# Summing the sixteen planes of the next batch's keys: plain loads with adds on GpSimd and VectorE in place of accumulating transfers

## Chip, core and metric

One core of a Trainium2 chip. The metric is the device time of one execution in microseconds (us); three runs of the kernel before took 972.6 to 973.67 us, median 973.59. PE is TensorE, DVE is VectorE, ACT is ScalarE, POOL is GpSimd, SP is SyncE (which here only issues transfers).

## What is computed

The reference, cut to what matters. B = 4 batches of N = 12288 queries, C = 128 channels, 768 pooled keys per batch; then a soft mixture of experts over all 49152 rows.

```python
kv_pool = kv.reshape(B, H // 4, 4, W // 4, 4, C).mean(axis=(2, 4))   # 16 planes are averaged
k = v = kv_pool.reshape(B, -1, C) @ w_sr                             # 768 keys per batch
s = scale * (q @ k.transpose(0, 2, 1)); a = softmax(s); x = a @ v    # attention
logits = x @ phi                                                     # 32 slots
d = softmax over rows of logits; slot_input = d.T @ x
slot_out = expert MLP of slot_input                                  # 8 experts, 1024 wide
out = softmax over slots of logits @ slot_out
```

## The kernel before

Queries are worked in **tiles** of 128, 12 tiles to a **group** (G), 8 groups and so 96 tiles (TB) to a batch, 32 groups in all. Per tile PE makes the scores `s` from keys and queries that are split into a high and a low part (`khi`, `klo`, `qhi`, `qlo`: three matmuls for each half of the 768 keys, lines 385 to 387), DVE takes the row maximum (391), ACT the exponential `p` (400). Half of `p` is transposed on DVE (424), half is split into two 16-bit parts by ACT (407) and POOL (411) into a buffer `hl` and transposed by a DMA that SP issues (420, tile `pb`). Per group PE turns the transposed `p` into logits (456, then 468, which needs `pb`), and, once the group's weights `D` have come through POOL, ACT and POOL (546, 562, 570), multiplies `p` by them (585: 96 matmuls in six blocks T0 to T5). The logits of 16 groups stay in one tile `LL`; the first 16 groups' logits are spilled by SP after use.

**Keys of a batch.** The 16 planes of 128x768 numbers are summed, and the sum gives `khi`/`klo` through PE (268), ACT (271) and DVE (275), the tables `us`, `vu`, `vb` and `selb` for the logits through PE (283), DVE (290 to 294), ACT (299) and so on, a transposition `put` on PE (312), and `V96` through PE (328) and ACT (331). This is the key stage, `kv_ops`. Batch 0's planes are loaded at the start and added by DVE (`add0`, `sum0`, `fin0`). For batches 1 to 3 `kv_acc` works while the batch ahead is being computed: SP loads plane 0 into two free slots of `LL`, and POOL issues fifteen transfers of 384 KB, one for each further plane, that add to what lies there; each waits until the one before it has landed.

**Order.** PE, DVE, ACT and POOL run their instructions in the order in which the plan emits them. Every operation has a key, the tile count `at` of its group plus a number from the table `TAU` for its kind, raised to just above the keys of what it depends on, and operations are emitted by ascending key. One unit of the key is one tile. SP's transfers go out in emission order too. In the table of before `kv1` to `kv15` lie between 24.91 and 91.518 of a batch's 96 units and `kmm0`, the key stage's first matmul, at 95.981, on the border to the next batch.

```python
    def op(self, eng, kind, at, deps, fn, acq=(), use=()):
        key = at + TAU.get(kind, 0.0)
        for d in deps:
            key = max(key, self.ops[d][2] + 1e-4)
```

Scores, key matmuls and logits share three buffers of two PSUM banks each (`ss`, ring "s").

Of the kernel before, what the change touches and what calls it, by code (L numbers as in the profile page):

```python
# [14 lines left out]
ALU = mybir.AluOpType  # L15
# [40 lines left out]
    "mcol": 21.441, "mmm": 21.883, "csum7": 22.133, "mred": 22.329, "dsub": 22.579, "xho12": 22.858, "dexp": 23.18,  # L56
# [3 lines left out]
    "xho15": 30.893, "bsum": 31.358, "kv3": 31.519, "dal": 31.805, "xh8": 31.827, "umax": 32.854, "csub": 33.213,  # L60
# [988 lines left out]
```

## Time and profile before

| what | value |
|---|---|
| median of three runs | 973.59 us |
| the profiled execution's own time | 982.6 us |
| its span, first to last instruction | 980.8 us |
| busy: PE, DVE, ACT, POOL | 873.0, 788.5, 661.3, 659.9 us |
| POOL's accumulating issues | 45, 41.1 us of POOL |
| queue that SP feeds / that POOL feeds, share of 16 DMA engines | 71.7% / 12.0% |

The span has three stages: the start until the first group is through (73 us), 30 further groups until 853 us, and the end with the experts and the output. "Busy" of PE counts matmuls that overlap one another; how fast PE goes is read from when instructions start. The profiled execution is 9.0 us longer than the median of the runs without a profile.

### The profile page before, as it was taken

How to read it: one execution, taken by the hardware profiler on the slowest of the kernel's cores; microseconds unless marked ns; L12 is line 12 of the kernel's file. 1: busy time of each engine (PE TensorE's matmuls, PEld its weight loads, DVE VectorE, ACT ScalarE, POOL GpSimd, SP SyncE). 2: the span in 40 equal slices, each digit the busy share in tenths (PEclk: the TensorE clock that was granted, in tenths of full speed). 3: DMA queues.
4: the chain of work that ended last, by engine and by line, in shares of the span. 5: the costliest groups of instructions: out<-in, count | busy, mean ns of one | idle time of the engine just before them, and what ended most of it. 6: DMA issues, size and time to landing. Idle time of an engine off the chain costs nothing. (4 is left out here: it accounts for less than half of the span.)

```text
span 980.8 us, 27134 instructions
## 1 busy us (share of the span) xinstructions
PE 873.0 (89%) x10436; PEld 618.0 (63%) x10436; DVE 788.5 (80%) x1496; ACT 661.3 (67%) x1244; POOL 659.9 (67%) x795
## 2 busy tenths in 40 slices
PE   1789998998998999998999999989999999866763
PEld 1677675775776766666767767757777777632341
DVE  6778886887887787887888878868998888847665
ACT  1677776776886776776877777857877888711333
POOL 0468886785788786785777877866776777747400
PEclk9999998999999999999999999999999999978567
DMA  7379999697789999895699999885666767693788
GB/s 300 64 147 179 178 174 171 130 169 136 132 160 171 166 178 163 146 163 101 143 179 175 166 176 151 159 142 104 133 130 129 131 130 131 107 335 161 319 347 362
DMA packets 338289, 167.61 MB, mean 171 GB/s; under 512 B 310768, under 2 KB 313072, under 8 KB 338032
## 3 DMA queue, kind: packets, MB, share of 16 engines
q1 hardware_dynamic: 331248, 148.04, 71.7%
q0 software_dynamic: 6480, 17.70, 12.0%
q8 instruction: 82, 1.34, 0.6%
q14 instruction: 47, 0.39, 0.1%
q10 hardware_dynamic: 432, 0.15, 0.1%
HBM read 62.01 MB, written 28.31 MB: 92 GB/s over the span
## 5 line engine op out<-in xcount | busy, mean ns | idle before, releaser
L411 POOL TENSOR_TENSOR hl<-p,hl 128x384 f16<-128x384 f32 x384 | 353.3, 962 | 97.1 <-issue 52.5
L400 ACT ACTIVATE p<-s,nm 128x768 f32<-128x768 f32 x384 | 344.5, 897 | 105.6 <-DVE nm L392 100.8
L391 DVE TENSOR_REDUCE nm<-s 128x1 f32<-128x768 f32 x384 | 364.4, 949 | 48.6 <-PE s L387 48.0
L385 PE MATMUL s<-khi,qhi 128*128 128x384 f32 x768 | 284.3, 370 | 7.3 <-ACT p L400 7.3
L387 PE MATMUL s<-khi,qlo 128*128 128x384 f32 x768 | 261.2, 340 | 0.1
L386 PE MATMUL s<-klo,qhi 128*128 128x384 f32 x768 | 260.8, 340 | 0.0
L385 PEld LDWEIGHTS s<-khi,qhi 128*128 128x128 f32 x768 | 146.0, 190 | 83.9 <-issue 65.2
L424 DVE STREAM_TRANSPOSE pa<-p 128x768 f32<-128x768 f32 x192 | 179.3, 958 | 0.0
L407 ACT ACTIVATE hl<-p 128x768 f16<-128x768 f32 x192 | 158.1, 836 | 29.5 <-DMA pb<-hl 25.1
L585 PE MATMUL m<-p,D 128*32 128x192 f32 x3072 | 168.0, 340 | 6.8 <-POOL D L570 4.4
L369 POOL TENSOR_TENSOR qlo<-q,qhi 128x512 fp32r<-128x512 f32 x96 | 132.4, 1379 | 56.6 <-ACT qhi L365 55.5
L386 PEld LDWEIGHTS s<-klo,qhi 128*128 128x128 f32 x768 | 146.6, 191 | 0.1
L387 PEld LDWEIGHTS s<-khi,qlo 128*128 128x128 f32 x768 | 146.2, 190 | 0.4 <-POOL qlo L369 0.4
L585 PEld LDWEIGHTS m<-p,D 128*32 128x32 f32 x3072 | 82.9, 111 | 67.0 <-issue 30.2
L456 PE MATMUL lq<-pa,vu 32*32 32x384 f32 x3072 | 88.5, 491 | 1.9 <-DVE pa L424 1.9
L400 ACT ACTIVATION_READ_ACCUMULATOR p<-s,nm 128x1 f32 x384 | 74.2, 193 | 0.0
L392 DVE TENSOR_SCALAR nm<-nm 128x1 f32<-128x1 f32 x384 | 59.1, 154 | 13.2
L479 DVE COPY lps<-lq 128x768 f32<-128x768 f32 x32 | 30.6, 958 | 47.8 <-PE lq L468 47.8
L468 PE MATMUL lq<-pb,vb 128*32 128x384 f16 x1152 | 54.7, 334 | 15.8 <-DMA pb<-hl 8.6
L456 PEld LDWEIGHTS lq<-pa,vu 32*32 32x32 f32 x3072 | 45.5, 103 | 32.5 <-issue 14.0
L365 ACT ACTIVATE qhi<-q 128x512 fp32r<-128x512 f32 x96 | 59.7, 621 | 2.0 <-PE s L386 2.0
L979 PE MATMUL po<-ct,sl 32*128 32x384 f32 x192 | 38.7, 739 | 24.5 <-DVE ct L973 24.1
(120 smaller groups left out, 736.5 us busy)
## 6 DMA issues: line engine op xcount, KB each, us to landing
q<-qT SPq DMA_DIRECT2D x96, 256.0 KB, 3.3
outT<-o SPq DMA_DIRECT2D x32, 768.0 KB, 4.4
LL<-kvT POOLq DMA_DIRECT2D x45, 384.0 KB, 6.1
raw<-kv SPq DMA_DIRECT2D x8, 768.0 KB, 11.6
pb<-hl SPq DMA_TRANSPOSE x384, 3.6
w_p<-w SPq DMA_DIRECT2D x6, 768.0 KB, 6.6
pa<-w SPq DMA_DIRECT2D x1, 3328.0 KB, 15.4
spill<-LL SPq DMA_DIRECT2D x16, 192.0 KB, 2.1
```

The lines of the kernel that those rows point to most:

```text
L365: nc.scalar.activation(qsp[i][0], src, AF.Copy)
L369: nc.gpsimd.tensor_tensor(out=lo, in0=src, in1=hi.bitcast(F32), op=ALU.subtract)
L385: nc.tensor.matmul(s, hi[:, qc], khi[:, k], start=True, stop=False)
L386: nc.tensor.matmul(s, hi[:, qc], klo[:, k], start=False, stop=False)
L387: nc.tensor.matmul(s, lo[:, qc], khi[:, k], start=False, stop=True)
L391: nc.vector.tensor_reduce(out=NM[t], in_=S[t][:, :, :HK], axis=XY, op=ALU.max, negate=True)
L400: nc.scalar.activation(PP[t // 2][:, t % 2, :].rearrange("p (h n) -> p h n", h=2), S.pop(t)[:, :, :HK], AF.Exp, bias=NM.pop(t), scale=1.0, ...
L407: nc.scalar.activation(HL[k][:, :, 0, :], PP[k][:, :, KA:], AF.Copy)
L411: nc.gpsimd.tensor_tensor(out=hl[:, 1, :], in0=PP[t // 2][:, t % 2, KA:], in1=hl[:, 0, :], op=ALU.subtract)
L424: nc.vector.transpose(out=PA[:, n, :, o : o + 2, :].rearrange("p n a i -> p a n i"), in_=PP[k][:, :, :KA].rearrange("p a (n j) -> p a n j" ...
L456: nc.tensor.matmul(lp(g, c, r), VU[b][rows, kb, :], PA[rows, halves(g), kb, :, :], start=(k == 0), stop=False, skip_group_check=True)
L585: nc.tensor.matmul(d["pst"][c * Q32 : (c + 1) * Q32, :KW], d["D"][:, t, :], pp[:, u, c * KW : (c + 1) * KW], start=(t == 0), stop=(t == G ...
```

## The change

`kv_acc` is gone. All sixteen planes come by plain loads that SP issues (`kv_load`): plane 0 into the two `LL` slots of before, the others by turns into two more pairs of free slots (`plane(b, 0)` and `plane(b, 1)`). They are added to plane 0 by `kv_add`: planes 3, 7, 11 and 15 by DVE in one instruction of 128x768 (`kd`), the other eleven by POOL in two instructions of 128x384 each (`ka`). For batches 2 and 3 the first load waits for the spills of six groups in place of two. All numbers of `TAU` are new, so that every engine's order changes, in the start and the end as well.

```diff
-    def kv_acc(b, c):
-        dst, src = kvb(b), kvT[b - 1, :, c, :]
+    def kv_load(b, c):
         if c == 0:
-            nc.sync.dma_start(out=dst, in_=src)
-            PO[b] = dst
-        else:
-            nc.gpsimd.dma_start(out=dst, in_=src, accum_op=ALU.add, max_dma_last_dim=4 * NK)
+            PO[b] = plane(b, 2)
+        nc.sync.dma_start(out=plane(b, 2 if c == 0 else c % 2), in_=kvT[b - 1, :, c, :])
+
+    def kv_add(b, c, h, eng):
+        k = slice(h * HK, (h + 1) * HK) if h is not None else slice(0, NK)
+        eng.tensor_tensor(out=PO[b][:, k], in0=PO[b][:, k], in1=plane(b, c % 2)[:, k], op=ALU.add)
...
-        first = [pool0[0], pool0[1], ops["s", t]] + ([ops["sp", (nb - 2) * GPB + KVS + i] for i in range(2)] if nb > 1 else [])
-        a = op("SP", "kv0", t, first, lambda: kv_acc(nb, 0), acq=[("kv", nb)])
+        first = [pool0[0], pool0[1], ops["s", t]] + ([ops["sp", (nb - 2) * GPB + i] for i in range(6)] if nb > 1 else [])
+        acc = op("SP", "kv0", t, first, lambda: kv_load(nb, 0), acq=[("kv", nb)])
+        prev = [acc]
         for c in range(1, R2):
-            a = op("POOL", f"kv{c}", t, [a], lambda c=c: kv_acc(nb, c), use=[("kv", nb)])
-        kv_ops(nb, t, [[a], [a]], [("kv", nb)])
+            ck = (f"ks{c % 2}", (nb, c))
+            ld = op("SP", f"kv{c}", t, first, lambda c=c: kv_load(nb, c), acq=[ck])
+            if c % 4 == 3:
+                prev = [op("DVE", f"kd{c}", t, [ld] + prev, lambda c=c: kv_add(nb, c, None, nc.vector), use=[ck, ("kv", nb)])]
+            else:
+                prev = [
+                    op("POOL", f"ka{2 * c + h}", t, [ld, prev[h % len(prev)]], lambda c=c, h=h: kv_add(nb, c, h, nc.gpsimd), use=[ck, ("kv", nb)])
+                    for h in range(2)
+                ]
+        kv_ops(nb, t, [prev, prev], [("kv", nb)])
...
 TAU = {
...
```

By the new keys, for the keys of batch 2 (units from the start of batch 1): loads between 17 and 75, POOL's 22 adds at 26 to 75 (6, 4, 3, 5 and 4 of them in the third to seventh group), DVE's at 36, 49, 66 and 79, the matmul of the tables at 79, those of the keys at 86, `V96`'s at 147.

**POOL, while batch 0 runs** (lines 411 and 369 are the splits of `p` and `q`, 261 the accumulating issue). Before:

```order
L261 DMA LL<-kvT 128x768
L369 TENSOR_TENSOR qlo_703<-q_620,qhi_702 128x512
L411 TENSOR_TENSOR hl_666<-p_631,hl_666 128x384
L411 TENSOR_TENSOR hl_727<-p_683,hl_727 128x384 x2
L369 TENSOR_TENSOR qlo_769<-q_663,qhi_768 128x512
L500 TENSOR_SCALAR r_395<-r_395 128x12
L261 DMA LL<-kvT 128x768
L411 TENSOR_TENSOR hl_819<-p_706,hl_819 128x384 x2
L411 TENSOR_TENSOR hl_882<-p_756,hl_882 128x384 x2
L411 TENSOR_TENSOR hl_909<-p_796,hl_909 128x384
L261 DMA LL<-kvT 128x768
L411 TENSOR_TENSOR hl_909<-p_796,hl_909 128x384
```
After, in the fourth group (the same lines are 419 and 377; 269 is an add of two planes, xN counts neighbours alike):

```order
L419 TENSOR_TENSOR hl_994<-p_886,hl_994 128x384 x2
L554 TENSOR_TENSOR D_1043<-LL,gm_1028 128x384
L578 TENSOR_TENSOR D_1043<-D_1043,ri_942 128x384
L419 TENSOR_TENSOR hl_1026<-p_980,hl_1026 128x384
L377 TENSOR_TENSOR qlo_1058<-q_975,qhi_1057 128x512
L269 TENSOR_TENSOR LL<-LL 128x384 x2
L562 TENSOR_TENSOR da_1099<-gm_671,gm_1028 128x32
L419 TENSOR_TENSOR hl_1026<-p_980,hl_1026 128x384
L419 TENSOR_TENSOR hl_1115<-p_1045,hl_1115 128x384 x2
L269 TENSOR_TENSOR LL<-LL 128x384 x3
L612 TENSOR_TENSOR LL<-LL,RM 128x384
```
Three issues to a group have become two to six adds, between the same neighbours.

**PE, end of batch 0** (`pk` key matmuls, `pu` tables, `put` transposition, `s` scores; 585 is a T block). Before:

```order
L585 MATMUL m<-p_2083,D_2512 32x192 x8
L585 MATMUL m<-p_2146,D_2512 32x192 x8
L268 MATMUL pk_2897<-LL,w_sb 128x384
L283 MATMUL pu_2899<-LL,wp_92 128x384 x2
L268 MATMUL pk_2897<-LL,w_sb 128x384
L312 MATMUL put_2917<-ident,us_2910 128x128 x3
L385 MATMUL s_2924<-khi_2895,qhi_2793 128x384
L386 MATMUL s_2924<-klo_2896,qhi_2793 128x384
```
After, first some fifty rows earlier than the second piece, then the keys and the transposition:

```order
L394 MATMUL s_2446<-klo_132,qhi_2377 128x384
L395 MATMUL s_2446<-khi_131,qlo_2378 128x384
L291 MATMUL pu_2453<-LL,wp_92 128x384 x2
L493 MATMUL m<-lps_2318,selb_163 32x384 x4
L393 MATMUL s_2473<-khi_131,qhi_2377 128x384
L394 MATMUL s_2473<-klo_132,qhi_2377 128x384
```

```order
L593 MATMUL m<-p_1873,D_2556 32x192 x8
L276 MATMUL pk_2656<-LL,w_sb 128x384 x2
L393 MATMUL s_2663<-khi_131,qhi_2570 128x384
L394 MATMUL s_2663<-klo_132,qhi_2570 128x384
L395 MATMUL s_2663<-khi_131,qlo_2571 128x384
L393 MATMUL s_2663<-khi_131,qhi_2570 128x384
L394 MATMUL s_2663<-klo_132,qhi_2570 128x384
L395 MATMUL s_2663<-khi_131,qlo_2571 128x384
L593 MATMUL m<-p_1900,D_2556 32x192 x8
L320 MATMUL put_2685<-ident,us_2503 128x128 x3
L393 MATMUL s_2692<-khi_131,qhi_2570 128x384
```
The key stage stood in one piece between the last block of the old batch and the first score that needs the new keys; now scores of the old batch stand between its parts, and other rows too between them and the new batch.

**The start, batch 0's own keys.** PE before, then after (`pv` gives `V96`, line 328 before and 336 after):

```order
L199 MATMUL m<-phi_sb,wT_sb 128x32
L268 MATMUL pk_133<-pooled_129,w_sb 128x384
L328 MATMUL pv_144<-w_sb,pooled_129 96x128 x8
L268 MATMUL pk_133<-pooled_129,w_sb 128x384
L283 MATMUL pu_166<-pooled_129,wp_92 128x384 x2
L385 MATMUL s_179<-khi_131,qhi_159 128x384
L386 MATMUL s_179<-klo_132,qhi_159 128x384
```

```order
L206 MATMUL m<-phi_sb,wT_sb 128x32
L276 MATMUL pk_133<-pooled_129,w_sb 128x384 x2
L291 MATMUL pu_154<-pooled_129,wp_92 128x384 x2
L336 MATMUL pv_170<-w_sb,pooled_129 96x128 x8
L393 MATMUL s_181<-khi_131,qhi_148 128x384
L394 MATMUL s_181<-klo_132,qhi_148 128x384
L395 MATMUL s_181<-khi_131,qlo_149 128x384
```
And DVE before, then after, where it adds the second half's planes (`raw`), from the end of the first half on:

```order
L217 TENSOR_TENSOR raw_4_116<-raw_4_116 128x768
L221 TENSOR_TENSOR raw_0_114<-raw_0_114,raw_4_116 128x768
L217 TENSOR_TENSOR raw_8_118<-raw_8_118 128x768
L221 TENSOR_TENSOR raw_0_114<-raw_0_114,raw_8_118 128x768
L217 TENSOR_TENSOR raw_12_120<-raw_12_120 128x768
L221 TENSOR_TENSOR raw_0_114<-raw_0_114,raw_12_120 128x768
L227 TENSOR_TENSOR pooled_129<-raw_0_114 128x384
L275 SCALAR_TENSOR_TENSOR klo_132<-pk_133,khi_131 128x384 x2
```

```order
L228 TENSOR_TENSOR raw_0_106<-raw_0_106,raw_12_112 128x768
L234 TENSOR_TENSOR pooled_129<-raw_0_106 128x384
L283 SCALAR_TENSOR_TENSOR klo_132<-pk_133,khi_131 128x384
L224 TENSOR_TENSOR raw_0_114<-raw_0_114 128x768
L224 TENSOR_TENSOR raw_4_116<-raw_4_116 128x768
L228 TENSOR_TENSOR raw_0_114<-raw_0_114,raw_4_116 128x768
L224 TENSOR_TENSOR raw_8_118<-raw_8_118 128x768
```
Both `pv` parts now stand between `pu` and the first score, and DVE's first `klo` ahead of the second half's adds.

## Rows read from the trace of the kernel before

**Rows 1.** Windows: us; busy us of PE, PEld, DVE, ACT, POOL; PEclk; DMA share; GB/s.

```profile
73.43:257.18 183.75, 174.28 (x2165) 124.59 (x2164) 153.34 (x289) 136.98 (x260) 141.13 (x163) 0.98 0.95 160
257.18:472.06 214.88, 202.53 (x2526) 146.41 (x2527) 175.94 (x332) 158.29 (x301) 159.54 (x185) 0.98 0.94 156
472.06:681.37 209.31, 200.66 (x2526) 145.24 (x2527) 176.59 (x335) 158.10 (x303) 159.56 (x185) 0.99 0.90 155
681.37:853.45 172.08, 171.33 (x2204) 124.29 (x2204) 152.58 (x289) 136.53 (x262) 127.31 (x149) 1.00 0.69 127
805.19:829.32 24.13, 24.13 (x311) 17.44 (x312) 21.46 (x40) 19.39 (x37) 18.30 (x22) 1.00 0.74 126
226.01:257.18 31.17, 27.62 (x322) 19.14 (x323) 24.95 (x49) 21.78 (x41) 18.59 (x22) 1.00 0.68 132
956.30:980.80 24.50, 8.47 (x66) 4.18 (x64) 12.92 (x20) 7.50 (x10) 1.07 (x2) 0.79 0.89 363
```
**Rows 2.** Groups by line and shape: times run | busy us, mean ns | idle before.

```profile
L411 POOL TENSOR_TENSOR hl<-p,hl 128x384 f16<-128x384 f32 x384 | 353.3, 962 | 97.1 <-issue 52.5 <-ACT hl L407 33.1 <-ACT da L566 9.5
...
L261 POOL DMA_DIRECT2D LL<-kvT x45 | 41.1, 914 | 15.0 <-DMA LL<-kvT 13.3 <-DMA pb<-hl 1.7
...
L513 POOL TENSOR_TENSOR LL<-LL,ri 128x384 f32<-128x384 f32 x32 | 27.3, 852 | 25.3 <-DVE LL L494 16.0 <-DVE LL L497 9.0
...
L221 DVE TENSOR_TENSOR raw<-raw,raw 128x768 f32<-128x768 f32 x6 | 5.7, 956 | 0.2
```
**Rows 3.** DMA, groups 1 to 7: queue's packets, MB, share; issues, KB each, landing us.

```profile
q0 software_dynamic: 2160, 5.90, 22.1%
...
LL<-kvT POOLq DMA_DIRECT2D x15, 384.0 KB, 6.4
...
pb<-hl SPq DMA_TRANSPOSE x85, 4.3
```
**Rows 4.** DMA issues, groups 24 to 30 (no accumulates): KB each, median us to landing.

```profile
pb<-hl SPq DMA_TRANSPOSE x85, 2.9
```
**Rows 5.** DMA issues of the whole span: the plain loads of plane 0.

```profile
LL<-kvT SPq DMA_DIRECT2D x3, 384.0 KB, 3.5
```
**Rows 6.** Waits of the whole span: us in total, times, longest.

```profile
ACT hl L407 <- DMA pb<-hl: 25.1, 15, 3.4
```
**Rows 7.** Timeline, PE, end of batch 0: start us, us, instruction, [idle before].

```profile
227.15 0.91 PE L268 MATMUL pk<-LL,w_sb 128*128 128x384 f32 x2
...
228.97 1.56 PE L283 MATMUL pu<-LL,wp 128*128 128x384 f32 x4 [0.91 <-ACT p L400]
...
233.73 0.55 PE L312 MATMUL put<-ident,us 128*128 128x128 f32 x3 [2.18 <-ACT us L299]
```
**Rows 8.** Timeline, PE, in group 28: score tiles and a T block.

```profile
782.97 0.45 PE L385 MATMUL s<-khi,qhi 128*128 128x384 f32 x1
...
784.26 0.86 PE L585 MATMUL m<-p,D 128*32 128x192 f32 x16
...
785.68 0.34 PE L385 MATMUL s<-khi,qhi 128*128 128x384 f32 x1
...
786.74 0.34 PE L385 MATMUL s<-khi,qhi 128*128 128x384 f32 x1
```
**Rows 9.** Timeline of the start, PE.

```profile
16.42 1.65 PE L268 MATMUL pk<-pooled,w_sb 128*128 128x384 f32 x2 [8.14 <-DVE pooled L227]
...
17.86 1.92 PE L328 MATMUL pv<-w_sb,pooled 128*96 128x128 f32 x8
```
**Rows 10.** Timeline of the start, ACT.

```profile
20.30 0.48 ACT L271 ACTIVATE khi<-pk 128x384 fp32r<-128x384 f32 x1
...
30.43 0.90 ACT L299 ACTIVATE us<-pu,am 128x768 f32<-128x768 f32 x1 [1.98 <-PE s L387]
```
**Rows 11.** Timeline of the start, DVE.

```profile
23.43 0.55 DVE L275 SCALAR_TENSOR_TENSOR klo<-pk,khi 128x384 fp32r<-128x384 f32 x1
...
31.87 0.92 DVE L391 TENSOR_REDUCE nm<-s 128x1 f32<-128x768 f32 x1
```

More of the change, by code (lines that the diff above doesn't have):

```diff
@@ L26 @@
 TAU = {
[29 rows of a table removed]
-    "mcol": 21.441, "mmm": 21.883, "csum7": 22.133, "mred": 22.329, "dsub": 22.579, "xho12": 22.858, "dexp": 23.18,
[3 rows of a table removed]
-    "xho15": 30.893, "bsum": 31.358, "kv3": 31.519, "dal": 31.805, "xh8": 31.827, "umax": 32.854, "csub": 33.213,
[16 rows of a table removed]
[33 rows of a table added]
+    "mred": 22.025, "dsub": 22.255, "csum15": 22.486, "dexp": 22.864, "dmul": 23.176, "csum17": 23.472, "T0": 23.703,
[23 rows of a table added]
 }
@@ L135, in attention_then_soft_moe @@
         "s": 3, "T": 1, "x": 1, "p": 13, "pa": 3, "pb": 3, "hl": 3, "q": 2, "qs": 2, "lps": 1, "g": 3, "D": 2,
-        "kv": 2, "K": 2, "V": 1, "c": 16, "o": 1,
+        "kv": 2, "ks0": 1, "ks1": 1, "K": 2, "V": 1, "c": 16, "o": 1,
     }
@@ L161, in attention_then_soft_moe, with plane @@
     flat = LL.rearrange("p k t s -> p (k t s)")
-    def kvb(b):
-        o = ((b % 2) * (NSL // 2) + KVS) * G * NS
+    def plane(b, n):
+        o = ((b % 2) * (NSL // 2) + 2 * n) * G * NS
         return flat[:, o : o + NK]
```

104 rows, old and new, of the table TAU are left out of this document.

## The prediction

> **What bounds the kernel now.** I read the windows first, cut at the start of the slot maximum (line 530) of one group after another, so that a window of n groups has n periods [rows 1]. The reader is to look at PE's column. In groups 24 to 30, when no keys are being summed, PE is busy for 171.33 of 172.08 us, and a single group such as 805.19 to 829.32 takes 24.13 us with PE busy throughout and DVE at 21.46: PE's instruction stream is the bound, and 24.13 us is the floor of a group. The three stretches before it hold 7, 8 and 8 groups and take 183.75, 214.88 and 209.31 us. Over the floor that is 14.8, 21.8 and 16.3 us, with 3.2 us in the last: 56.1 us over 30 groups.
>
> Where do they go? One place is seen at once: the group in which a batch ends, 226.01 to 257.18, takes 31.17 us, 7.0 over the floor, with PE idle for 3.5 of it. The timeline there [rows 7] shows the key stage in one piece, from 227.15 to the transposition at 233.73: PE waits 0.91 us for a PSUM buffer and 2.18 us for `us`, since nothing else stands in its order. The other place is where accumulates run. The DMA queues show it [rows 3, 4]: POOL's queue has 22.1% of the engines' time in groups 1 to 7, each accumulate lands after 6.4 us, and the transposes that PE's second logits part (line 468) waits for land after a median of 4.3 us, where it is 2.9 without accumulates. ACT waits 25.1 us for transposes to free `hl` [rows 6], which delays POOL's split and the next transposes in turn.
>
> **The change part by part.** *Accumulates removed.* 22.1% of 183.75 us over 15 transfers is 2.7 us of all 16 engines for each [rows 3]. A plain load of 384 KB has no row for its engine time; in the output stretch the engines move 363 GB/s at a share of 0.89 [rows 1], so 393 kB would take 0.96 us, an estimate from that row. The lower end is that, the upper end 2.7 us, no gain; I take 1.0, since that row is plain too. Three loads per group then take 3 us of DMA in place of 8, and the share falls from 0.95 to about 0.8, nearer to the 0.69 at which stalls are absent.
>
> The Trainium skill speaks against part of this (DMA: Bandwidth & Descriptors, Queues, rings and completion order): a DMA engine takes turns between queue rows packet by packet and takes one row's descriptors in ring order. By that rule a plain load in SP's own queue stands in front of the transposes issued after it, where the accumulate took turns with them. No row here shows a load ahead of a transpose; what it would cost, up to 1 us for each load, is less than the 1.4 us by which the medians differ.
>
> *POOL.* Removed per batch: 15 issues of 0.914 us and 15.0 us / 3 of idle time ahead of them, 18.7 us [rows 2]. Added: 22 adds of 128x384. The nearest row is the multiply of the same shape and types on POOL, 852 ns; the split with a 16-bit operand takes 962 [rows 2]: 18.7 to 21.2 us, so POOL's own work is even. New is the wait for a load. A plain load lands after 3.5 us [rows 5]; by the new keys loads 5, 6, 8, 9 and 14 are issued only 0.3 to 1 unit ahead of their first add, 0.6 to 2 us at 24.13 / 12 = 2.0 us for a unit, so that POOL, in order, may wait up to 2.9 us at five places per batch, 0 to 14 us. Queued behind such an add are the splits `lo`, whose transposes the logits need. POOL has 24.13 - 18.30 = 5.8 us free in a group [rows 1]; 4.4 adds with waits of 0.5 us each take 6.0. So I let each of the 15 groups with adds lose 0.5 us, 7.5 in all; the ends are 0 and 1.5 each.
>
> *DVE.* Twelve adds of 128x768, 956 ns [rows 2], one in a group at most, against 24.13 - 21.46 = 2.7 us free [rows 1]: nothing. Without that cover it is 11.5 us.
>
> A second rule of the Trainium skill (SBUF — State Buffer, Who interferes with whom) speaks against the change: a VectorE instruction with two SBUF inputs and a GpSimd instruction that reads SBUF lock each other out for a whole instruction. The row of 956 ns is from the start, where POOL did nothing, so no row shows it either way.
>
> *Key stage spread.* The PE work in it stays: two `pk` of 0.91, `pu` 1.56, `put` 0.55 [rows 7], 3.9 us per batch, 11.8 in all. The stage of `V96` stays too; it is most of the 3.2 us of the last stretch, and comes three times, 9.6. Of 56.1 us, 34.7 can go. What is late next: `pu`, `pk` and `put` each hold one of the three PSUM buffers while scores go on, through a DVE and an ACT step; one score tile may wait at each, and I charge 1.2 us per batch, 3.5 in all (0 to 3 us per batch). That leaves 34.7 - 7.5 - 3.5 = **23.7 us gained**.
>
> *Order of the T blocks.* A score tile between two T blocks takes 784.26 - 782.97 = 1.29 us from start to start, one among its like 786.74 - 785.68 = 1.06 [rows 8]. In the new order T4 and T5 stand together, one such switch fewer per group: 0.23 us x 30 is 6.9; where PE waits anyway it is nothing, so **5 us gained**.
>
> *The start.* DVE now has `klo` of the first half ahead of the second half's adds. It needs `pk` (16.42 + 1.65) and `khi` (0.48), and takes 0.55, so it ends near 19.1 [rows 9 to 11]. The second half's adds, which went on at about 16.3, when DVE had released that `pk`, come 2.8 us later, and the second `pk` with them. One `pv` part of 1.8 us no longer stands ahead of the second `pk`, so `us`, at 30.43 before, comes 1.0 us later and ends at 32.3. Then ACT frees the first `pv` part (0.6) and PE makes the second (1.9), which now stands ahead of the first score: score done near 36.0, first row maximum at 36.1 where it was 31.87. That is **4.2 us lost** (0 to 6). The end keeps its instructions in another order; I take 0, plus or minus 2.
>
> Sum: 23.7 + 5.0 - 4.2 = 24.5 us. Against the profiled execution's own time that is 982.6 - 24.5 = 958.1. The median of the runs, 973.59, is 9.0 us lower; the same step gives **949 us**. If all 9.0 us were stalls of the kind removed, the runs would gain only 15.5 and take 958, which the range holds.
>
> **Rivals.**
> 1. POOL becomes the bound: waits for landing add up and every group with adds loses 1.5 us more. For it: 5.8 us free against up to six adds in one group. Against: before, three issues and their waits took as much. 949 + 15 = 964.
> 2. DVE's adds and POOL's instructions shut each other out. Each of 12 DVE adds then costs POOL 0.96 us where it has nothing free: 949 + 11.5 = 960. The chance is small, since nothing in the trace bears it out. This is the lock that the Trainium skill states (SBUF — State Buffer, Who interferes with whom).
> 3. The loads slow the transposes as the accumulates did, so that the change doesn't relieve DMA. Then only the boundaries gain, 3 x (7.0 - 3.9 - 1.2) = 5.7, and the T blocks: 973.6 - 5.7 - 5.0 + 4.2 = 967.
> 4. Slower: the place is POOL's adds with their waits. The gain of 24.5 is gone when the 15 groups lose 1.6 us more each, 2.1 in all; that needs 5.8 + 2.1 = 7.9 us for 4.4 adds, 1.8 us per add with its wait. At 2.2 us it is 9.7 per group, 3.9 lost, 949 + 51 = 1000; at 2.0 it is 987. Half of this needs every add to wait 1 us; a landing of 5 us or more in SP's queue would do it.
>
> **How the numbers follow.** Forecast 0.50, rival 1 0.20, rival 2 0.10, rival 3 0.06, rival 4 0.14. Faster by over 0.2% (2 us, about what a measurement of this kernel can tell from no change) takes all but rival 4 and the edges of 1 and 3: 0.82; within it 0.05; slower 0.13. The low end, 934, is no residual stall (11 us) and no loss in the start (4); the high end, 969, takes in rivals 1 to 3 and leaves out rival 4.
>
> **What would show it.** Right: windows of groups 1 to 23 at 24 to 25 us, boundary groups at about 28 to 29; median landing of transposes near 3.2 us; the first row maximum at about 36 us; POOL's adds at 0.85 us each; undisturbed groups at 23.9. Wrong: POOL idle ahead of line 269 for more than 12 us per batch, adds of well over 1 us on DVE or POOL beside each other, waits of PE ahead of line 476 (468 before) in groups with adds, or transposes still landing after 4.3 us.

## The result and the profile after

The changed kernel takes 962.96 us (median of four runs, 960.92 to 975.94) where the kernel before takes 973.63: a ratio of 0.9878, 95% interval 0.9848 to 0.9907. In a second comparison it was 0.9883 (0.9822 to 0.9944). So 10.7 us were gained, where the forecast said 24.5.

At the end of the program PE runs at one of two granted clocks, which differ from execution to execution of the same kernel and move the time by some 12 us; the recorded execution of the changed kernel with 975.94 us is of the longer sort, so what follows shows another recorded execution of it (961.80 us), and compares kernels by groups 1 to 30 first, which that doesn't touch.

The windows of that execution, cut at the slot maximum (now line 538) as in [rows 1]: groups 1 to 7, 8 to 15, 16 to 23, 24 to 30, and one undisturbed group.

```profile
core 0: us, PE busy (x) PEld busy (x) DVE busy (x) ACT busy (x) POOL busy (x), PEclk, DMA share, GB/s
76.68:252.93 176.25, 170.66 (x2164) 123.05 (x2162) 155.63 (x294) 138.36 (x261) 151.52 (x170) 1.00 0.86 166
252.93:457.41 204.48, 198.43 (x2525) 143.88 (x2525) 178.48 (x337) 159.33 (x301) 169.68 (x191) 1.00 0.85 164
457.41:662.71 205.30, 198.45 (x2525) 143.59 (x2525) 178.50 (x339) 160.01 (x302) 169.76 (x192) 1.00 0.79 156
662.71:838.24 175.53, 170.87 (x2204) 124.56 (x2204) 152.27 (x289) 137.84 (x261) 127.18 (x148) 1.00 0.69 123
789.57:813.94 24.37, 23.96 (x310) 17.51 (x310) 21.75 (x41) 19.77 (x38) 18.29 (x21) 1.00 0.75 132
```

Against [rows 1] the first three stretches are 7.5, 10.4 and 4.0 us shorter, but the last, which has neither accumulates nor loads, is 3.5 us longer, and a group that nothing disturbs takes 24.30 us (24.29 to 24.37) where it took 24.13. PE is no longer busy throughout in it. The timeline of PE shows why, at the two T blocks that now stand together (lines 1 and 2), ahead of the next score tile (line 3):

```profile
start us, us, engine line op out<-in xcount [idle before <-releaser]
788.65 0.86 PE L593 MATMUL m<-p,D 128*32 128x192 f32 x16
789.92 0.86 PE L593 MATMUL m<-p,D 128*32 128x192 f32 x16 [0.41 <-DVE gm L538]
790.71 0.44 PE L393 MATMUL s<-khi,qhi 128*128 128x384 f32 x1
```

The second block waits 0.41 us for VectorE to read the slot maximum `gm`; from the start of the first block to the start of the score tile it is 790.71 - 788.65 = 2.06 us. PE's waits as a list (us in total, times, the longest) have it in nearly every group; in the kernel before the same wait came 5 times, 2.1 us in all.

```profile
PE m L593 <- DVE gm L538: 12.8, 31, 0.4
```

The DMA issues of groups 1 to 7 answer to [rows 3]: one hardware queue, loads that land after 3.7 us, transposes after 3.3 where it was 4.3 beside accumulates (and 3.0 now in groups 24 to 30).

```profile
q1 hardware_dynamic: 73078, 28.86, 85.2%
...
LL<-kvT SPq DMA_DIRECT2D x15, 384.0 KB, 3.7
...
pb<-hl SPq DMA_TRANSPOSE x84, 3.3
```

The key stage, spread over groups 5 and 6 of a batch (times on PE, batch 3), answers to [rows 7]: the same work with one wait of 0.58 us, where 0.91 and 2.18 stood. The boundary group is 24.3 us long, groups 5 and 6, which hold the stage now, 26.2 and 26.9.

```profile
604.14 1.53 PE L291 MATMUL pu<-LL,wp 128*128 128x384 f32 x4
...
619.83 0.91 PE L276 MATMUL pk<-LL,w_sb 128*128 128x384 f32 x2
621.32 0.91 PE L276 MATMUL pk<-LL,w_sb 128*128 128x384 f32 x2 [0.58 <-ACT khi L279]
624.00 0.55 PE L320 MATMUL put<-ident,us 128*128 128x128 f32 x3
```

At the start, the first row maximum begins at 35.14 us, where [rows 11] has it at 31.87:

```profile
35.14 0.96 DVE L399 TENSOR_REDUCE nm<-s 128x1 f32<-128x768 f32 x1 [3.73 <-PE s L395]
```

### The profile page after: what moved, and what is told of

It is laid out like the page before. It is cut to its first block, busy times and chain, and to the rows that moved or that the text cites. A ratio compares the mean times of both kernels' runs of the same rounds, so it can differ in the third digit from the quotient of the medians.

```text
span 974.2 us, 27117 instructions
## 1 busy us (share of the span) xinstructions
PE 870.9 (89%) x10436; PEld 618.1 (63%) x10436; DVE 794.8 (82%) x1508; ACT 666.1 (68%) x1244; POOL 690.0 (71%) x816
## 5 line engine op out<-in xcount | busy, mean ns | idle before, releaser
L419 POOL TENSOR_TENSOR hl<-p,hl 128x384 f16<-128x384 f32 x384 | 347.7, 924 | 38.2 <-ACT hl L415 24.8
L393 PE MATMUL s<-khi,qhi 128*128 128x384 f32 x768 | 280.8, 366 | 8.5 <-ACT p L408 7.5
L432 DVE STREAM_TRANSPOSE pa<-p 128x768 f32<-128x768 f32 x192 | 182.3, 962 | 0.0
L593 PE MATMUL m<-p,D 128*32 128x192 f32 x3072 | 166.4, 337 | 16.5 <-DVE gm L538 12.8
L377 POOL TENSOR_TENSOR qlo<-q,qhi 128x512 fp32r<-128x512 f32 x96 | 125.4, 1306 | 31.1 <-ACT qhi L373 31.1
L612 POOL TENSOR_TENSOR LL<-LL,RM 128x384 f32<-128x384 f32 x32 | 26.6, 833 | 68.2 <-DVE RM L609 68.2
L269 POOL TENSOR_TENSOR LL<-LL 128x384 f32<-128x384 f32 x66 | 66.1, 1011 | 7.8 <-DVE LL L269 4.1
L996 PE MATMUL po<-ct,sl 32*128 32x384 f32 x192 | 47.2, 895 | 23.8 <-DVE ct L990 23.3
L485 ACT ACTIVATE lps<-lq 128x768 f32<-128x768 f32 x32 | 26.0, 814 | 56.5 <-PE lq L476 56.5
```

The lines of the kernel that those rows point to most:

```text
L269: eng.tensor_tensor(out=PO[b][:, k], in0=PO[b][:, k], in1=plane(b, c % 2)[:, k], op=ALU.add)
L377: nc.gpsimd.tensor_tensor(out=lo, in0=src, in1=hi.bitcast(F32), op=ALU.subtract)
L393: nc.tensor.matmul(s, hi[:, qc], khi[:, k], start=True, stop=False)
L419: nc.gpsimd.tensor_tensor(out=hl[:, 1, :], in0=PP[t // 2][:, t % 2, KA:], in1=hl[:, 0, :], op=ALU.subtract)
L432: nc.vector.transpose(out=PA[:, n, :, o : o + 2, :].rearrange("p n a i -> p a n i"), in_=PP[k][:, :, :KA].rearrange("p a (n j) -> p a n j" ...
L593: nc.tensor.matmul(d["pst"][c * Q32 : (c + 1) * Q32, :KW], d["D"][:, t, :], pp[:, u, c * KW : (c + 1) * KW], start=(t == 0), stop=(t == G ...
```

## Experiments

All kernels, with the length of groups 1 to 30 in the recorded execution (slot maximum of group 0 to that of group 30, by the windows), the start of group 0, and the time:

| kernel | group 0 at | groups 1 to 30 | median of runs | ratio to before (95%) |
|---|---|---|---|---|
| before, two recorded executions | 73.43; 71.38 | 780.02; 771.18 | 973.6 to 976.8 | |
| changed, once more | 76.68 | 761.56 | 962.94 | 0.9883 (0.9822 to 0.9944) |
| sixth T block behind a score tile | 75.99 | 781.22 | 991.28 | 1.0106 (1.0043 to 1.0169) |
| sixth T block emitted earlier | 76.75 | 777.05 | 982.68 | 1.0087 (1.0046 to 1.0127) |
| PSUM tile split | 74.42 | 747.40 | 955.35 | 0.9796 (0.9725 to 0.9866) |
| start of before | 70.50 | 762.32 | 962.73 | 0.9841 (0.9776 to 0.9906) |
| end of before | 74.64 | 762.50 | 969.37 | 0.9965 (0.9918 to 1.0012) |
| accumulates in the new order | 76.71 | 810.96 | 1017.62 | 1.0461 (1.0371 to 1.0551) |
| the same, issued early | 81.47 | 868.92 | 1080.38 | 1.1109 (1.1038 to 1.1179) |
| loads and adds in the old order | 69.74 | 784.18 | 980.84 | 1.0104 (1.0056 to 1.0153) |
| the same, all adds on VectorE | 74.53 | 804.68 | 1000.43 | 1.0211 (1.0146 to 1.0276) |
| key stage in one piece | 77.47 | 778.38 | 984.50 | 1.0129 (1.0068 to 1.019) |
| changed, without loads and adds | 77.21 | 755.83 | 965.69 | 0.9842 (0.9763 to 0.992) |
| before, without accumulates | 69.88 | 754.66 | 955.60 | 0.9761 (0.9694 to 0.9828) |
| split, and start of before | 71.90 | 748.87 | 944.40 | 0.9703 (0.9657 to 0.9749) |

**The changed kernel once more.** No edit.

> The changed kernel once more, unaltered, beside the kernel before: the reference for the three kernels run with it. If the 11 us of the first comparison are the change's own, the ratio is 0.988 again (a gain of 11 to 12 us). If that figure was thinned by disturbed runs and the 24.5 us of the forecast are there, the ratio is 0.975. The profile should again show groups that nothing disturbs at 24.30 us and the start of group 30 about 15 us earlier than in the kernel before.

The gain is the change's own: 12.7 us by these medians.

**The T blocks.** Three kernels ask what became of the forecast's 5 us. First the blocks apart, as before:

```diff
-    "T5": 34.214, "tacc": 35.207,
+    "T5": 34.8, "tacc": 35.42,
```

> The changed kernel with the fifth and sixth T block apart, as in the kernel before: the score tile s0 stands between them again, and the row maximum m0 ahead of the sum of T. Theory: in the changed kernel the sixth T block stands right behind the slot maximum's product on PE and waits for VectorE to read it (0.5 us per group), so undisturbed groups go back from 24.30 to 24.13 us and the kernel gains 0.17 x 30 = 5 us over the changed one. Rival: the floor rose for another reason (engines slowed by the adds, the new places of the splits); then groups stay at 24.3 us and the time within 1 us. The forecast's own term says that it loses 5 to 7 us, since one switch more costs 0.23 us per group.

Theory and rival are both refuted: undisturbed groups take 24.85 us. PE's timeline, in a group with neither adds nor loads:

```profile
811.48 0.86 PE L593 MATMUL m<-p,D 128*32 128x192 f32 x16 [0.76 <-DVE acc L604]
```

This is the next group's first T block. It needs the one buffer of T, which VectorE reads (`tacc`) after the sixth block; in the new order it comes too soon for that. Second, the blocks together, the sixth emitted ahead of VectorE's read:

```diff
-    "T5": 34.214,
+    "T5": 34.01,
```

> The changed kernel with its fifth and sixth T block adjacent as they are, but with the sixth emitted ahead of the slot maximum's read on VectorE, so that it doesn't wait for it. This is the forecast's term by itself. If the forecast's 0.23 us per switch is right and only the wait ate it, T4 to T5 takes 0.8 us from start to start, undisturbed groups 23.9 us, and the kernel gains 0.40 x 30 = 12 us over the changed one. Rival: the read of the slot maximum now waits for the sixth block instead, and all that hangs on it (the differences, their exponentials, the next T block) comes 0.8 us later; if that is on the path, groups stay at 24.3 us or more and nothing is gained.

```profile
807.55 0.86 PE L593 MATMUL m<-p,D 128*32 128x192 f32 x16 [0.98 <-POOL D L578]
...
827.50 1.51 PE L593 MATMUL m<-p,D 128*32 128x192 f32 x32
```

The rival holds: 32 matmuls run in one piece in 1.51 us, but the read of the slot maximum, with its differences and exponentials, comes behind them, and the first T block waits 0.98 us for POOL's product `D`. Groups take 24.73 us. Third, the shared tile. `m` has two PSUM banks, the T blocks in one, the slot maximum and others in the other. They never touch the same numbers, but a wait is set for the tile:

```diff
-    mt = pm.tile([P, 2, 512], F32, tag="m", name="m")
+    mx = pm.tile([P, 512], F32, tag="mx", name="mx")
+    mT = pm.tile([P, 512], F32, tag="mT", name="mT")
```

> The changed kernel with the PSUM tile that the T blocks share with the slot maximum split in two tiles of one bank each; no order is changed, only that the sixth T block no longer waits for VectorE to read the slot maximum, nor the read for the block (16 evictions at the very end become two each, since they used the tile as one). Theory: the forecast's step on the T blocks was right but for this wait; undisturbed groups go from 24.30 to 23.9 us, and the kernel gains 12 us over the changed one, less what the evictions cost at the end. Rival: with the first T block of the next group only two score tiles behind, the chain from the slot maximum over its differences to that block binds as soon as the wait is gone; then groups end at 24.2 to 24.3 us and 0 to 3 us are gained.

```profile
797.24 0.48 PE L534 MATMUL mx<-ident,cm 128*128 128x128 f32 x2
797.65 1.51 PE L594 MATMUL mT<-p,D 128*32 128x192 f32 x32
```

```profile
774.43:798.14 23.71, 23.71 (x318) 17.58 (x310) 21.66 (x42) 19.87 (x38) 18.34 (x22) 1.00 0.79 136
```

Undisturbed groups take 23.67 to 23.71 us with PE busy throughout, 0.42 under [rows 1], and groups 1 to 30 are 14.2 us shorter than in the changed kernel. The theory holds, and more than the forecast's 0.23 us per switch is there once the wait is gone. The starts on PE show it: the next score tile here, and in the kernel before one block of the pair and the score tile behind it:

```profile
799.09 0.45 PE L394 MATMUL s<-khi,qhi 128*128 128x384 f32 x1
```

```profile
804.26 0.86 PE L585 MATMUL m<-p,D 128*32 128x192 f32 x16
805.05 0.44 PE L385 MATMUL s<-khi,qhi 128*128 128x384 f32 x1
```

Apart, a block takes 0.79 us from start to start and the two 1.58; together they take 799.09 - 797.65 = 1.44, a gain of 0.14 that the forecast didn't count beside its 0.23. In the changed kernel they take 2.06: the wait costs 0.62 us a group there, more than the switch is worth.

**Start and end.** The keys of the start (all kinds `hk`, `hv` and `hu`) go back to the values of before, then those of the end (`csum`, `ceps`, `crec`, `cmul`, `x`, `wl`, `cb`); two of each:

```diff
-    "hklo0": -60.686, "hvmm0": -1.845,
+    "hklo0": -26.362, "hvmm0": -76.453,
```

> The changed kernel with the order of the start of the kernel before (first key stage: both klo behind the second half's adds, the first pv part between the two pk). Theory: the start of group 0 comes back from 76.89 to about 73.5 us and the kernel gains 3.4 us (the forecast said that the start loses 4.2). Rival: what the start loses is waited for again later, where the transposes or the first adds of the next batch's keys set the pace; then the time stays within 1 us.

```diff
-    "csum7": 2.641, "crec7": -141.588,
+    "csum7": 22.133, "crec7": -127.058,
```

> The changed kernel with the order of the end of the kernel before (sums of the slots, their reciprocals and products, the experts' layers, the loads of the weights). Theory: groups 1 to 30 stay as in the changed kernel (start of group 30 near 838.2 us), and what follows it shrinks from 121.8 us to about 117, so that the kernel gains 4 to 5 us over the changed one. Rival: the last group is longer (24.7 us where it was 21.5) for other reasons than the order of the end, such as later transposes; then less than 1 us is gained.

With the old start group 0 begins 6.2 us earlier, and group 30 is still 5.4 earlier. By the medians (962.73 against 962.94) the gain doesn't show, by the lowest runs (956.58 against 960.81) it is 4 us. The start varies by itself: over all kernels of the table but the one with early accumulates group 0 begins at 74.4 to 77.5 us with the new start (nine executions, the first of the changed kernel among them, mean 76.3) and at 69.7 to 74.5 with the old (seven, mean 71.6), 4.7 us apart. The old end shortens group 31 from 24.67 to 21.84 us, but no run is faster by it (lowest 961.89): a miss. The end's length goes by its clock. The windows of the output stage, and from group 30 on into the experts' layers, in two recorded executions of the same changed kernel, the one of 975.94 us first:

```profile
891.20:946.50 55.30, 39.99 (x194) 24.94 (x194) 35.73 (x61) 17.05 (x24) 13.67 (x21) 0.50 0.75 308
838.60:891.20 52.60, 33.90 (x444) 15.52 (x444) 28.75 (x88) 8.38 (x18) 29.18 (x57) 0.77 0.74 245
```

```profile
896.00:934.00 38.00, 21.35 (x176) 12.08 (x176) 30.70 (x46) 16.98 (x23) 9.01 (x12) 1.00 1.00 408
838.20:891.20 53.00, 32.70 (x446) 15.27 (x446) 29.44 (x91) 8.38 (x18) 30.10 (x58) 0.81 0.74 243
```

At a granted clock of 0.50 (1.2 GHz) the output stage moves 308 GB/s with the DMA engines busy for 0.75 of the time, at 1.00 (2.4 GHz) 408 with the engines full; from group 30 to the end it is 135.5 and 121.8 us. The stretch ahead of it looks alike in both: PE is busy for 33.90 of 52.60 and for 32.70 of 53.00 us. Recorded executions of like clock tell what the end's order is worth. Where 0.79 to 0.82 was granted over the whole end, it lasts 121.8 to 123.1 us in the new order (three, with the tile unsplit) and 122.4 to 123.5 in the old (three), so that the order is worth under 2 us either way. Where it was 0.61 to 0.64, it is 132.9 to 135.6 in the new (six) and 132.6 in the old (one).

**Accumulates or order?** The accumulates of before in the changed kernel, first at about their old places, then early:

```diff
-        acc = op("SP", "kv0", t, first, lambda: kv_load(nb, 0), acq=[("kv", nb)])
+        a = op("SP", "kv0", t, first, lambda: kv_acc(nb, 0), acq=[("kv", nb)])
+        for c in range(1, R2):
+            a = op("POOL", f"kv{c}", t, [a], lambda c=c: kv_acc(nb, c), use=[("kv", nb)])
```

> The changed kernel's order, key stage spread as it is, but the planes of the next keys come by accumulating transfers again, as in the kernel before (a little closer together, so that they end ahead of the key stage; no adds on GpSimd and VectorE). Theory: the accumulates cost about 18 us of stalls over three batches, so this kernel is 15 to 20 us slower than the changed one (977 to 982 us), with transposes landing after about 4.3 us and groups 1 to 4, 9 to 12 and 17 to 20 at 25 to 28 us. Rival: the gain came from the order and the spread key stage; then the time is within 4 us of the changed kernel's 962.

> The changed kernel's order with accumulating transfers again, this time issued early and at even distances (one per 4.7 row tiles, 9.6 us), so that the last one has landed well before the key stage. Theory (accumulates cost about 18 us of stalls over three batches whatever the order): group 30 starts 15 to 20 us later than the changed kernel's 838 us, and no group waits for the last accumulate as groups 5, 13 and 21 did in the first run of this kind (36 to 38 us each). Rival: the first run's loss of 49 us came from being late alone; then group 30 starts within 5 us of 838.

Both are far slower than either side expected, and neither isolates the accumulates: `pu` waits for the last of them 18.6 and 18.8 us in three batches, and in the second score tiles also wait 34.1 us for POOL. They tell only that this order with accumulates at these two sets of places is far slower. Then the loads and adds in the order of before:

```diff
 # TAU of the kernel before, but
+    "kv0": 19.496, "kv2": 22.024, "ka0": 4.5, "ka1": 6.0, "kd3": 35.651,
...
```

> The kernel before in its own order (key stage in one piece at the end of a batch, start and end as they were), but with plain loads and adds in place of accumulating transfers. Theory: the stalls of the accumulates go (18 us of the forecast's 23.7), the groups at the batch ends stay at 31 to 33 us; 973 - 18 = 955 us. With the order of before there is no loss at the start, the end or the T blocks. Rival: in this order GpSimd's adds stand in the way of the splits and give back most of it; then 965 us or more.

The rival holds: nothing is gained, the ratio is above 1, and groups 3, 11 and 19 take 29.3, 29.5 and 29.0 us. In group 3 POOL waits 2.23 us ahead of an add for VectorE's add, with splits queued behind, and PE then 3.33 us for a transposition:

```profile
127.79 1.02 POOL L269 TENSOR_TENSOR LL<-LL 128x384 f32<-128x384 f32 x1 [2.23 <-DVE LL L269]
```

```profile
138.87 3.07 PE L476 MATMUL lq<-pb,vb 128*32 128x384 f16 x36 [3.33 <-DMA pb<-hl]
```

All adds on VectorE instead (the four that were there move as well, the first from 35.651 to 16.8):

```diff
-            if c % 4 == 3:
+            if True:
```

> The kernel before in its own order with plain loads, as in the earlier run, but with all 15 adds of a batch on VectorE and none on GpSimd. Theory: in the earlier run GpSimd waited up to 2.2 us for VectorE's adds with the splits queued behind, and PE then waited up to 3.4 us for the transposes; without adds on GpSimd groups 2, 3, 10, 11, 18 and 19 go from 26.7 to 29.5 us back to 24.5 to 26.8, and group 30 starts 8 us or more earlier, relative to group 0, than the earlier run's 784 us. Rival: VectorE has no room (2.7 us per group free against up to two adds of 0.96), and the time is no better.

The time is no better, as the rival has it, and groups 2, 8, 10, 16 and 18 take 29.8 to 31.8 us; groups 3, 11 and 19 do come back to 26.3, as the theory has it. But it isn't shown that VectorE has no room. Its waits for loads ahead of an add are five, one in each of the five long groups (the first line: us in total, times, longest); behind the longest, PE waits for the slot maximum:

```profile
DVE LL L269 <- DMA LL<-kvT: 16.2, 5, 5.5
...
513.70 0.96 DVE L269 TENSOR_TENSOR LL<-LL 128x768 f32<-128x768 f32 x1 [5.50 <-DMA LL<-kvT]
...
516.84 1.51 PE L593 MATMUL m<-p,D 128*32 128x192 f32 x16 [6.06 <-DVE gm L538]
```

VectorE runs in order, so what stands behind such an add waits for the load too. The run doesn't separate that from the time of the adds. Leaving the work out gives the prices by themselves, of loads and adds together and then of the accumulates:

```diff
     def kv_load(b, c):
+        if c:
+            return
...
     def kv_add(b, c, h, eng):
+        return
```

> The changed kernel without the 15 loads and 26 adds per batch of the next keys (the keys of batches 2 to 4 are those of one plane alone; all else keeps its place). What group 30 gains against the changed kernel is the full price of loads and adds. My reading of the trace (groups with adds are as long as the same groups of the last batch without) says 1 to 2 us in all: group 30 at 836 to 838 us. The forecast charged 7.5 us: group 30 at 831. If the adds are a hidden bound, 10 us or more.

```diff
-        else:
-            nc.gpsimd.dma_start(out=dst, in_=src, accum_op=ALU.add, max_dma_last_dim=4 * NK)
```

> The kernel before without its 15 accumulating transfers per batch (the keys of batches 2 to 4 are those of one plane alone; all else keeps its place). What group 30 gains against the kernel before (842.6 and 853.5 us in two profiled executions) is the full price of the accumulates in the old order. The forecast counted some 25 us of stalls by them (18 gained, 7.5 still charged): group 30 at 820 to 828 us, groups 1 to 4, 9 to 12 and 17 to 20 at 24.1 to 25 us, and the batch-end groups still at 30. Rival: the stalls are the old order's own; then group 30 stays above 835.

The windows of groups 1 to 30, of the changed kernel without loads and adds, then of the kernel before without accumulates:

```profile
77.21:833.04 755.83, 735.92 (x9418) 534.84 (x9416) 654.04 (x1245) 595.65 (x1125) 547.97 (x635) 1.00 0.73 132
```

```profile
69.88:824.54 754.66, 743.00 (x9418) 536.88 (x9416) 658.12 (x1243) 589.98 (x1124) 548.57 (x636) 1.00 0.72 132
```

Loads and adds cost 761.56 - 755.83 = 5.7 us; I had read 1 to 2 out of the trace. The accumulates cost 16.5 or 25.4 us, by the execution of before that one takes. Without either, both orders are equally long. Against the same 754.66 us, loads and adds in the old order cost 784.18 - 754.66 = 29.5 us. The issues of groups 1 to 7 of the changed kernel without loads also tell what the loads do to the transposes, which land after 3.3 us beside them:

```profile
pb<-hl SPq DMA_TRANSPOSE x86, 3.2
```

**Key stage in one piece.** Thirteen numbers go back to those of before, four of them shown:

```diff
-    "kmm0": 86.112, "umm": -35.066, "umax": 80.117, "ut": 86.97,
+    "kmm0": 95.981, "umm": 95.981, "umax": 32.854, "ut": -6.241,
```

> The changed kernel with the key stage of the next batch in one piece at the end of a batch, at the places of the kernel before; loads and adds stay. The forecast put the boundary's stalls that the spreading removes at 7.0 - 3.9 - 1.2 = 1.9 us per batch, 5.7 in all: groups 7, 15 and 23 go from 24.3 to about 31, groups 5, 6 (13, 14, 21, 22) from 26.2 and 26.9 to 24.3, and group 30 starts 5 to 7 us later. Rival: spreading is worth nothing by itself (its waits for PSUM are as long); then group 30 starts within 2 us of 838.

Spreading is worth 16.8 us here, three times what was expected: the boundary groups take 35.13, 33.96 and 32.37 us, the first two more than in the kernel before. The first and the third, and one line of PE in the third:

```profile
225.28:260.41 35.13, 30.47 (x321) 21.51 (x321) 24.93 (x49) 21.38 (x41) 18.50 (x22) 0.90 0.52 100
647.91:680.28 32.37, 27.17 (x321) 19.11 (x321) 24.78 (x49) 21.39 (x41) 18.50 (x22) 1.00 0.59 108
...
651.09 0.86 PE L593 MATMUL m<-p,D 128*32 128x192 f32 x16 [1.98 <-POOL D L578]
```

Two things add to the forecast's term. In each of the three a T block now stands ahead of the key stage, with no score tile of the new batch before it, and waits 1.98 us for `D`, 5.9 in all. And PE's clock: in the first, 0.90 is the mean of stretches at 0.50 and 1.00 (1.2 and 2.4 GHz), and PE is busy 3.3 us longer than in the third at 1.00, though its waits are alike (1.98 us and then 2.19 for `us`; 1.98 and 2.56 in the third). So the 16.8 us aren't the price of the one piece alone.

**The kernel before once more.**

> The kernel before, unaltered, profiled once more: its profiled execution took 9 us more than the median of its runs, and the granted clock in the output stage at the end was 0.50 there for two of nine slices. If those 9 us lie in that stage, a profiled run near 973 us has the same groups (group 30 at 853.5 us) and an end of about 117 us at a higher clock; if they are stalls of the groups, group 30 starts at about 845 us.

A run of 967.86 us, 14.7 below the execution of [rows 1]. Its groups 1 to 30:

```profile
71.38:842.56 771.18, 743.31 (x9418) 536.69 (x9416) 658.15 (x1243) 590.29 (x1124) 587.57 (x681) 1.00 0.88 152
```

They are 8.8 us shorter, 3.9 of it in the three boundary groups and the rest in others that have accumulates (groups 24 to 30 differ by under 0.1 us); the start is 2.1 and the end 3.8 us shorter. So most of it is the groups, and what they lose differs between executions.

**Both losses taken out:** split tile and old start.

> The changed kernel with both losses of the order taken out: the PSUM tile split as in the earlier run (undisturbed groups at 23.68 us) and the order of the start of the kernel before (start of group 0 at 70.5 us). If the two add up, group 30 starts at 821.8 - 6.2 + (76.7 - 74.4) = 817 to 818 us and the kernel is 4 us faster than with the split alone: runs at 945 to 951 us. Rival: the earlier start is waited for again; then the time stays at 950 to 955.

The edits are the two shown above. 944.40 us, the fastest version here, and its interval lies wholly under that of the changed kernel, though not under that of the split alone. But the two don't add up as expected: group 30 starts at 820.77 us, 1.1 earlier than with the split alone, since that execution had the earliest of the new starts, and groups 1 to 30 are 1.5 us longer here. The recorded executions are 10.9 us apart, and 9.8 of that lie in the end, which was granted 0.82 here and 0.63 there, so that most of the distance goes with the clock and not with the edit.

## Why the prediction was wrong, step by step

| term, us gained | forecast | shown |
|---|---|---|
| accumulates out | 25.5 (18.0 net and 7.5 charged) | 25.4; 16.5 in the other execution of before |
| loads and adds in | -7.5 | -5.7 |
| key stage, the rest within groups | 5.7 | 4.5 (754.66 - 755.83, with the 5.7 of the next line put back) |
| T blocks | 5.0 | -5.7 (0.19 x 30) |
| start | -4.2 | -3.3; -5.3 (-4.7 over all kernels) |
| end | 0 | 5.6; 1.8, by clock |

Where two figures stand, the first is from the profiled execution of before that the forecast was read from, the second from the other. The second figures sum to 6.1 (967.86 - 961.80 is 6.06); the first to 20.8, which is 982.6 - 961.8. The gain by the medians lies between. The key stage's 4.5 is what is left over, not measured by itself.

**The step that failed** is "In the new order T4 and T5 stand together, one such switch fewer per group ... so 5 us gained". The switch was there, and worth more than its price (0.42 us a group in the split kernel, where 0.23 was forecast), but the score tile that went from between them had hidden a wait: the sixth block comes behind the slot maximum in a PSUM tile that both use, and waits for VectorE to read it, which costs 0.62 us a group. The step costed the move from starts on PE alone and didn't ask what the moved instruction waits for. It is 10.7 us of the miss, from 5.0 gained to 5.7 lost.

**The base was too high.** "Against the profiled execution's own time" the stalls were 56.1 us; in the other execution of before they are 771.18 - 30 x 24.11 = 47.9. So the term of the accumulates was sized on one execution: 25.4 us there, 16.5 in the other, 9.0 under the forecast. The forecast took the sum off the median as well, and said what would follow if the 9.0 us between the two were stalls of the kind removed: 958. Between the two recorded executions 8.8 us are in the groups; where a run at the median loses its time no trace shows.

**What held, and what didn't.** Transposes land after 3.3 us (3.2 given), and the start lost 3.3 us by the first row maximum, where 4.2 was given. The signs named for being right failed elsewhere: groups 1 to 23 average 25.2 to 25.7 us (24 to 25 given), undisturbed groups take 24.30 (23.9), POOL's adds 1.01 (0.85), and the boundary groups 24.3, since the stage left them (28 to 29). Over their own floor the 30 groups keep 761.56 - 30 x 24.30 = 32.6 us, where the forecast left 56.1 - 23.7 = 32.4. That they agree is luck, for the parts were off against each other: without adds, groups 25 to 27 and their likes in other batches hold about 14 us and the key stage 13, where 9.6 and 15.3 were given. The end's 0, plus or minus 2, agrees with the 1.8 us at like clock.

**The rivals.** 1, POOL as the bound: not so, loads and adds cost 5.7 us in all, and POOL waits 7.0 us ahead of its adds in three batches (more than 12 in each would have shown it). 3, loads that slow the transposes as accumulates did: not so. In groups 1 to 7 transposes land after 3.3 us beside loads and after 3.2 in the same groups without them; beside accumulates it is 4.3, and 2.8 without. The Trainium skill's rule (DMA: Bandwidth & Descriptors, Queues, rings and completion order) that one ring's descriptors are taken in order would have the loads delay the transposes behind them; the traces show no more of it than that 0.1 us in the median. 4, slower: not here, but it is what the adds do in the order of before. 2, the lock between VectorE and GpSimd: I gave it a small chance, and its mechanism is there, see the last section; its price on the path is within the 5.7 us.

What stays open: why the clock of the end differs between executions of one kernel, why the lengths of groups with accumulates do, and whether the old order could have gained with the adds at other places.

## What to carry to other kernels

Before an instruction is moved, ask what it waits for at the new place, not only what it costs there: a neighbour that is taken away may have been hiding a wait, and two banks in one tile waited for each other as one here. A transport that is cheaper by itself may gain nothing until the order around it is made for it (adds in the old order: none). Make the sum of stalls from two executions of the kernel before: here they were 8.8 us apart in the groups. And look whether an engine that seems to have no room is not waiting for a load instead.

## What the runs showed of the hardware

In these traces an add of two SBUF operands on VectorE and an instruction on GpSimd that reads SBUF lock each other out. Instructions of three lines over the whole changed kernel (lowest, median and highest ns):

```profile
L269 POOL TENSOR_TENSOR LL<-LL x66: 998/1013/1036, 85.0 to 597.4; 128x384 f32<-128x384 f32 x66
...
L269 DVE TENSOR_TENSOR LL<-LL x12: 950/1046/1418, 104.2 to 603.0; 128x768 f32<-128x768 f32 x12
...
L377 POOL TENSOR_TENSOR qlo<-q,qhi x96: 1262/1286/2017, 27.3 to 829.3; 128x512 fp32r<-128x512 f32 x96
...
L508 POOL TENSOR_SCALAR r<-r x32: 228/234/943, 69.1 to 850.1; 128x12 f32<-128x12 f32 x32
```

The longest of the last two stand beside an add, as here, on VectorE and on POOL:

```profile
576.27 1.05 DVE L269 TENSOR_TENSOR LL<-LL 128x768 f32<-128x768 f32 x1
...
576.48 0.94 POOL L508 TENSOR_SCALAR r<-r 128x12 f32<-128x12 f32 x1
```

An instruction of 0.23 us lasts 0.94 and ends 0.1 us after the add. Beside 9 of the 12 adds an instruction of POOL is 0.7 us longer so, some 6 us in all; what of it reaches the path isn't measured apart from the 5.7 us. It goes the other way too: the three adds with no instruction of POOL beside them take 0.95 us, the nine others 1.02 to 1.42. This is the rule of the Trainium skill (SBUF — State Buffer, Who interferes with whom) that a VectorE instruction with two SBUF inputs contends with a GpSimd instruction that reads SBUF, and the trace agrees. POOL's adds themselves take 1.01 us, not the 0.85 of the multiply in [rows 2].
